# Twelve clamps of an int64-to-float32 decode, moved from VectorE to GpSimd

## The chip, the cores and the metric

The kernel runs on one core of a Trainium2 chip. Its engines are TensorE (PE in the profile; PEld is its weight load), VectorE (DVE), ScalarE (ACT), GpSimd (POOL) and SyncE (SP, which only issues transfers here). Each engine works through its own queue in order, and engines wait for one another by semaphores. The metric is the device time of one execution in microseconds, compared as the median of several runs.

## The reference, cut to what matters

Attention with a local band, global columns and distance biases (ALiBi), and behind it a two-layer MLP with a clipped gate:

```python
# q, k, v: (4, 8, 768, 64) float32; n_global 8, n_local 96; w_in (512, 2048), w_out (2048, 512)
scores = q @ k.T / 8 - slope[h] * dist      # masked to the band and the 8 global columns
a = softmax(scores); attn = a @ v
x = attn as (3072, 512)
h = x @ w_in
g = h * clip(h + 3, 0, 6) / 6
out = g @ w_out                             # float32, (3072, 512)
```

The weights reach the kernel as 64-bit words (float64 bits) of which the kernel makes float32 on the chip. This is the decoding that the change touches.

## The kernel before, in words

**Tiling.** The 3072 rows of x are eight blocks of 384 rows. In a block, attention is worked in four pairs of heads; pairs are numbered through all blocks, 0 to 31. The MLP of a block has 16 steps, f = 0 to 15, of 128 hidden units each. A step has two halves: twelve matmuls of 128x384 into the bank hp (L166), and nine of 128x512 into three accumulators (L198). Between the halves ScalarE and VectorE make the gate g (L177, L178), its high part gh (L186 on ScalarE, or L184 on GpSimd in later blocks) and the rest gl (L191). Each weight is kept as a high and a low part (w1h and w1l, w2h and w2l), hence three products per matmul.

**Weights.** They come in 32 chunks of 128x512 words, chunk 2f for the first half of step f and chunk 2f+1 for the second. A chunk's path is: a 512 KB transfer into a staging tile wst (L363, issued by SyncE); on ScalarE the magnitude of the high words, |high| into wz (L371); on GpSimd the low words scaled into we (L375); on VectorE the clamp of wz to the float32 exponents (L393), the mask and shift (L394), the sign (L402, which reads wst for the last time on VectorE), the sum with we (L408); on ScalarE the high part w1h or w2h (L412); on VectorE the low part w1l or w2l (L399). There are two buffers each of wst, wz and we, so the fetch of chunk i+2 waits for L402 and L375 of chunk i.

**The early part.** Blocks 0 to 2 get their attention (pairs 0 to 11) while the weights are decoded. Per pair: score matmuls (L809), distance and minimum on VectorE (L824), the exponentials on ScalarE (L828), sums on VectorE (L838, L839), division of the six row tiles n by their sums on GpSimd (L848; pair 0 on VectorE), transposes on TensorE (L856, L858) whose results ScalarE and VectorE copy to pt (L860), and the products with the values (L900) into one bank xp. ScalarE and VectorE bring that to xh (L152) and xl (L153); the next pair's L900 waits for xl, as there is one bank. From pair 8 on, steps f = 0 to 5 of block 0 stand between the pairs: hp of f0 ahead of pair 8's other transposes, and so on, f5 after pair 11's products. Then come steps 0 to 5 of block 1, steps 6 to 15 of blocks 0 and 1 in turn, and blocks 2 to 7, with the attention of the next block between their steps.

**What sets the order.** The generator `decode` yields after every part of a chunk with a price in microseconds of VectorE; `work` adds up the prices given to TensorE and to VectorE and takes further parts of the decoding as long as VectorE's account is the lower. That sets where in the program the parts stand. On TensorE, SyncE and GpSimd the queues keep program order (`in_order`); on VectorE and ScalarE a scheduler places the instructions. `magnitude(i + 1)` is called with L408 of chunk i.

```python
def work(self, pe, dve):
    self.given[0] += pe
    self.given[1] += dve
    while self.given[1] < self.given[0] and self.decoded < self.allowed:
        self.decode_step()
```

Of the kernel before, what the change touches and what calls it, by code (L numbers as in the profile page):

```python
# [9 lines left out]
F32 = mybir.dt.float32  # L10
# [4 lines left out]
ALU = mybir.AluOpType  # L15
# [23 lines left out]
LEAST, MOST = (float(np.uint32(e << 20).view(np.float32)) for e in (896, 1151))  # L39
# [10 lines left out]
FIRST = 6  # L50
# [8 lines left out]
class Kernel:  # L59
# [305 lines left out]
    def magnitude(self, i):  # L365


        words = self.raw[i].rearrange("p (c w) -> p c w", w=2)
        self.z[i] = self.zp.tile([P, DM], I32, name="wz")
        self.e[i] = self.ep.tile([P, DM], I32, name="we")  # L370
        self.nc.scalar.activation(out=self.z[i].bitcast(F32), in_=words[:, :, 1].bitcast(F32), func=AF.Abs)  # L371
        if i == 0:
            self.tc.add_manual_dep(self.nc.cur_bb.bb.instructions[-1], self.held, mybir.DependencyInfo(
                mybir.DependencyClass.NoSync, mybir.DependencyReason.DATA), reason="behind the first pairs")
        self.nc.gpsimd.tensor_scalar(out=self.e[i], in0=words[:, :, 0].bitcast(U32), scalar1=2.0 ** -29, scalar2=0.0, op0=ALU.mult, op1=ALU.add)  # L375

    def part(self, i, w1, w2):
        f = i // 2
        return (self.w1(w1, f), lambda a: a.rearrange("p (k c) -> p k c", k=NKT)) if i % 2 == 0 else (self.w2(w2, f), lambda a: a)

    def decode(self):

        nc = self.nc
        ts, stt, tt = nc.vector.tensor_scalar, nc.vector.scalar_tensor_tensor, nc.vector.tensor_tensor
        N = 2 * NF
        self.magnitude(0)
        for i in range(N + 1):
            a, b = i < N, i > 0  # L390
            if a:
                z = self.z[i]
                ts(out=z.bitcast(F32), in0=z.bitcast(F32), scalar1=LEAST, scalar2=MOST, op0=ALU.max, op1=ALU.min)  # L393
                ts(out=z, in0=z, scalar1=0x07FFFFFF, scalar2=3, op0=ALU.bitwise_and, op1=ALU.logical_shift_left)  # L394
            yield 0.68 * a
            if b:
                hi, sh = self.part(i - 1, self.w1h, self.w2h)
                lo, _ = self.part(i - 1, self.w1l, self.w2l)
                tt(out=lo, in0=sh(self.z.pop(i - 1).bitcast(F32)), in1=hi.bitcast(F32), op=ALU.subtract)  # L399
            yield 0.6 * b  # L400
            if a:
                stt(out=z, in0=self.raw[i].rearrange("p (c w) -> p c w", w=2)[:, :, 1], scalar=-0x40000000, in1=z,  # L402
                    op0=ALU.bitwise_and, op1=ALU.bitwise_or)
                if i + 2 < N:
                    self.fetch(i + 2)
            yield 0.6 * a
            if a:
                tt(out=z, in0=z, in1=self.e.pop(i), op=ALU.add)  # L408
                if i + 1 < N:
                    self.magnitude(i + 1)  # L410
                hi, sh = self.part(i, self.w1h, self.w2h)
                nc.scalar.copy(out=hi, in_=sh(z.bitcast(F32)))  # L412
            yield 0.69 * a
# [566 lines left out]
```

## Time and profile before

| What | Value |
|---|---|
| Median of three runs | 668.42 us (668.13 to 668.87) |
| The profiled execution's own time | 668.19 us |
| Its span, first to last instruction | 666.4 us |
| Granted TensorE clock | 0.999 |
| TensorE busy | 654.5 us, 98% of the span |
| VectorE busy | 423.4 us, 64% |
| ScalarE busy | 278.9 us, 42% |
| GpSimd busy | 219.9 us, 33% |

The span has 1.8 us less than the time of its execution; a change of the span is read as a change of the time. Busy time of TensorE is generous, since matmuls are pipelined and their ends are modelled; idle time is what is surely lost. The early part is told by stretches of 10 us, as the shares of the whole span say little of it. "SPq" rows are issues of transfers by SyncE, and the duration of such a row spans all its issues.

### The profile page before, as it was taken

What the parts mean: (1) busy time and instruction counts of PE and PEld (TensorE: products, weight loads), DVE (VectorE), ACT (ScalarE), POOL (GpSimd) and SP (SyncE); (2) the same over time, 40 slices, a digit from 0 to 9 for tenths busy, and PEclk for the clock granted to TensorE, in tenths of its full rate; (3) what the DMA queues carried; (4) which work ended last, traced back from release to release, by engine and by line L of the source; (5) the groups of instructions that cost most, each with busy time, mean ns of one, the idle gap of its engine ahead of it and who ended that gap; (6) DMA issues with size and microseconds to landing.
All of it is one profiled execution on the core that took longest, in us unless ns stands there. A gap on an engine that the chain in (4) does not pass through costs nothing.

```text
span 666.4 us, 11474 instructions
## 1 busy us (share of the span) xinstructions
PE 654.5 (98%) x3963; PEld 586.1 (88%) x3963; DVE 423.4 (64%) x1121; ACT 278.9 (42%) x736; POOL 219.9 (33%) x389
## 2 busy tenths in 40 slices
PE   9989999999999999999999999999999999999997
PEld 8768888888999999999999999899999999989995
DVE  6899999999234876366663886457662777422222
ACT  6898756555236333154324433143331444131111
POOL 5666622221000553043340444225340444302110
PEclk9999999999999999999999999999999999999999
DMA  8685644442003446625663366624555255510001
GB/s 288 179 253 195 198 150 135 153 134 94 1 1 134 135 139 184 174 81 138 164 154 131 86 179 164 173 80 126 155 152 137 80 150 147 138 48 2 1 1 53
DMA packets 60837, 84.74 MB, mean 127 GB/s; under 512 B 8416, under 2 KB 45536, under 8 KB 60768
## 3 DMA queue, kind: packets, MB, share of 16 engines
q1 hardware_dynamic: 60480, 83.64, 43.3%
q8 instruction: 33, 0.54, 0.3%
q14 instruction: 36, 0.29, 0.1%
q10 hardware_dynamic: 288, 0.26, 0.1%
HBM read 62.92 MB, written 20.97 MB: 126 GB/s over the span
## 4 chain that ended last, share of the span: by engine, by line
PE 81%; DVE 9%; ACT 3%; DMA 3%; issue 2%; POOL 1%; SPq 0%; ACTq 0%; DVEq 0%; POOLq 0%
PE hp L166 36%; PE acc L198 33%; DMA wst<-w 3%; PE xp L900 2%; PE sp L813 2%; PE tp L900 2%; PE tp L813 2%; ACT n L828 2%; DVE wz L402 2%; DVE wz L408 1%; DVE n L824 1%; DVE wz L394 1%; PE sp L198 1%; PE tp L198 1%; PE xp L198 1%
## 5 line engine op out<-in xcount | busy, mean ns | idle before, releaser
L177 ACT ACTIVATE g<-hp,small 128x384 f32<-128x384 f32 x127 | 73.5, 579 | 251.5 <-PE hp L166 231.9
L166 PE MATMUL hp<-xh,w1h 128*128 128x384 f32 x512 | 174.1, 340 | 0.8 <-ACT w1h L412 0.7
L166 PE MATMUL hp<-xh,w1l 128*128 128x384 f32 x512 | 172.9, 338 | 0.1
L166 PE MATMUL hp<-xl,w1h 128*128 128x384 f32 x512 | 172.0, 336 | 0.0
L184 POOL TENSOR_SCALAR gh<-g 128x384 fp32r<-128x384 f32 x96 | 51.6, 538 | 292.6 <-DVE g L178 257.4
L198 PE MATMUL acc<-w2h,gl 128*128 128x512 f32 x336 | 133.0, 396 | 0.1
L198 PE MATMUL acc<-w2l,gh 128*128 128x512 f32 x336 | 132.4, 394 | 0.0
L198 PE MATMUL acc<-w2h,gh 128*128 128x512 f32 x336 | 132.0, 393 | 0.0
L178 DVE SCALAR_TENSOR_TENSOR g<-g,hp 128x384 f32<-128x384 f32 x128 | 69.7, 544 | 86.7 <-ACT g L177 86.5
L848 POOL TENSOR_SCALAR n<-n,sums 128x232 f32<-128x232 f32 (+1 forms) x186 | 101.7, 562 | 35.7 <-DVE sums L839 21.3
L191 DVE TENSOR_TENSOR gl<-g,gh 128x384 fp32r<-128x384 f32 x128 | 78.6, 614 | 50.0 <-POOL gh L184 45.3
L828 ACT ACTIVATE n<-n,least 128x232 f32<-128x232 f32 (+1 forms) x192 | 89.1, 466 | 45.1 <-DVE least L824 43.9
L166 PEld LDWEIGHTS hp<-xh,w1h 128*128 128x128 f32 x512 | 96.3, 188 | 6.6 <-issue 1.4
L166 PEld LDWEIGHTS hp<-xl,w1h 128*128 128x128 f32 x512 | 96.2, 188 | 3.9
L166 PEld LDWEIGHTS hp<-xh,w1l 128*128 128x128 f32 x512 | 96.0, 188 | 0.4 <-DVE w1l L399 0.4
L198 PEld LDWEIGHTS acc<-w2h,gl 128*128 128x128 f32 x336 | 63.0, 187 | 14.7 <-DVE gl L191 1.0
L198 PEld LDWEIGHTS acc<-w2h,gh 128*128 128x128 f32 x336 | 63.3, 188 | 10.3 <-POOL gh L184 0.3
L198 PEld LDWEIGHTS acc<-w2l,gh 128*128 128x128 f32 x336 | 63.2, 188 | 10.3
L873 DVE STREAM_TRANSPOSE blocks<-n 128x256 f32<-128x256 f32 x112 | 43.5, 424 | 31.0 <-POOL n L848 18.7
L375 POOL TENSOR_SCALAR we<-wst 128x512 int32<-128x512 uint32 x32 | 27.8, 868 | 68.6 <-DMA wst<-w 52.2
L784 POOL TENSOR_SCALAR kx<-load 64x504 fp32r<-64x504 f32 (+1 forms) x40 | 31.0, 776 | 37.5 <-PE hp L166 35.9
L824 DVE CUSTOM_DVE_ANT_0 n<-sp,d 128x232 f32<-128x232 f32 (+1 forms) x70 | 23.6, 374 | 29.5 <-PE sp L813 29.0
(110 smaller groups left out, 780.9 us busy)
## 6 DMA issues: line engine op xcount, KB each, us to landing
wst<-w SPq DMA_DIRECT2D x32, 512.0 KB, 3.5
load<-pairs SPq DMA_DIRECT2D x22, 636.0 KB, 5.2
there<-blocks SPq DMA_DIRECT2D x52, 256.0 KB, 2.6
load<-pairs SPq DMA_DIRECT2D x32, 384.0 KB, 3.9
weights<-there SPq DMA_DIRECT2D x48, 192.0 KB, 3.8
out<-o SPq DMA_DIRECT2D x23, 256.0 KB, 2.1
weights<-there SPq DMA_DIRECT2D x32, 160.0 KB, 3.2
load<-pairs SPq DMA_DIRECT2D x9, 444.0 KB, 3.6
```

The costliest lines, as they stand in the source:

```text
L166: self.nc.tensor.matmul(hp, lhsT=self.w1(w, f)[:, kt, :], rhs=a[:, kt, :], start=(n == 0), stop=(n == 3 * NKT - 1))
L177: nc.scalar.activation(out=g, in_=hp, func=AF.Relu, bias=self.three, scale=1.0)
L178: nc.vector.scalar_tensor_tensor(out=g, in0=g, scalar=6.0, in1=hp, op0=ALU.min, op1=ALU.mult)
L184: self.nc.gpsimd.tensor_scalar(out=gh, in0=g, scalar1=1.0, scalar2=0.0, op0=ALU.mult, op1=ALU.add)
L191: self.nc.vector.tensor_tensor(out=gl, in0=g, in1=gh.bitcast(F32), op=ALU.subtract)
L198: self.nc.tensor.matmul(acc[tt], lhsT=a[:, tk], rhs=self.w2(w, f), start=(f == 0 and j == 0), stop=(f == NF - 1 and j == 2))
L375: self.nc.gpsimd.tensor_scalar(out=self.e[i], in0=words[:, :, 0].bitcast(U32), scalar1=2.0 ** -29, scalar2=0.0, op0=ALU.mult, op1=ALU.add)
L784: nc.gpsimd.tensor_scalar(out=part["kx"][own, c], in0=k[own, c], scalar1=1.0, scalar2=0.0, op0=ALU.mult, op1=ALU.add)
L824: nc.vector.tensor_tensor_reduce(out=e[:, j, lo:W], in0=sp[j][:, lo:W], in1=d, op0=ALU.add, op1=ALU.min, scale=scale, scalar=3.0e38, accum ...
L828: nc.scalar.activation(out=e[:, j, lo:W], in_=e[:, j, lo:W], func=AF.Exp, bias=self.least[:, i:i + 1], scale=-1.0, accum_out=self.sums[:, ...
L848: nc.gpsimd.tensor_scalar(out=e[:, j, lo:W], in0=e[:, j, lo:W], scalar1=over, scalar2=0.0, op0=ALU.mult, op1=ALU.add)
L873: nc.vector.transpose(out=blocks[:, :, s].rearrange("p b j q -> p j b q"), in_=e[:, :, c:c + P].rearrange("p j (b q) -> p j b q", b=4))
```

## The change

For the chunks i < 12 the clamp is no longer L393 on VectorE but a GpSimd instruction right behind the scaling of the low words (L378 in the new numbering), with the two bounds taken in the other order (minimum first). The price that `decode` yields for its first part falls from 0.68 to 0.34 for these chunks. Everything behind L375 gets line numbers 6 or 7 higher: L393, L394, L399, L402, L408 and L412 become L400, L401, L406, L409, L415 and L419; L824, L838, L839, L848 and L900 become L831, L845, L846, L855 and L907.

```diff
         self.nc.gpsimd.tensor_scalar(out=self.e[i], in0=words[:, :, 0].bitcast(U32), scalar1=2.0 ** -29, scalar2=0.0, op0=ALU.mult, op1=ALU.add)
+        if self.helped(i):
+            z = self.z[i].bitcast(F32)
+            self.nc.gpsimd.tensor_scalar(out=z, in0=z, scalar1=MOST, scalar2=LEAST, op0=ALU.min, op1=ALU.max)
+
+    def helped(self, i):
+        return i < 2 * FIRST
...
                 z = self.z[i]
-                ts(out=z.bitcast(F32), in0=z.bitcast(F32), scalar1=LEAST, scalar2=MOST, op0=ALU.max, op1=ALU.min)
+                if not self.helped(i):
+                    ts(out=z.bitcast(F32), in0=z.bitcast(F32), scalar1=LEAST, scalar2=MOST, op0=ALU.max, op1=ALU.min)
                 ts(out=z, in0=z, scalar1=0x07FFFFFF, scalar2=3, op0=ALU.bitwise_and, op1=ALU.logical_shift_left)
-            yield 0.68 * a
+            yield (0.34 if self.helped(i) else 0.68) * a
```

The lower price moves the decoding forward in the program. TensorE's order stays as it was. Three places show the rest.

GpSimd, from the chunks ahead of pair 10's division (n) to that of pair 11, before:

```order
L375 TENSOR_SCALAR we<-wst 128x512 x2
L848 TENSOR_SCALAR n<-n,sums 128x128 x2
L848 TENSOR_SCALAR n<-n,sums 128x232 x4
L375 TENSOR_SCALAR we<-wst 128x512 x2
L848 TENSOR_SCALAR n<-n,sums 128x128 x2
L848 TENSOR_SCALAR n<-n,sums 128x232 x4
```

and from the last chunk ahead of pair 10's division in the change:

```order
L375 TENSOR_SCALAR we<-wst 128x512
L378 TENSOR_SCALAR wz<-wz 128x512
L855 TENSOR_SCALAR n<-n,sums 128x128 x2
L855 TENSOR_SCALAR n<-n,sums 128x232 x4
L375 TENSOR_SCALAR we<-wst 128x512
L378 TENSOR_SCALAR wz<-wz 128x512
L375 TENSOR_SCALAR we<-wst 128x512
L378 TENSOR_SCALAR wz<-wz 128x512
L375 TENSOR_SCALAR we<-wst 128x512
L378 TENSOR_SCALAR wz<-wz 128x512
L855 TENSOR_SCALAR n<-n,sums 128x128 x2
L855 TENSOR_SCALAR n<-n,sums 128x232 x4
```

Before, chunks 4 and 5 stood ahead of pair 10 and chunks 6 and 7 ahead of pair 11. Now chunks 5 and 6 stand ahead of pair 10 (the first of them is not shown) and chunks 7, 8 and 9 ahead of pair 11, each with its clamp.

SyncE, the fetches of chunks (wst) and the value loads of pairs 11, 12 and 13 (768 wide), before:

```order
L290 DMA load_167<-pairs 128x768
L363 DMA wst<-w 128x1024 x2
L290 DMA load_72<-pairs 128x768
L363 DMA wst<-w 128x1024 x2
L290 DMA load_73<-pairs 128x768
L363 DMA wst<-w 128x1024 x21
```

and in the change:

```order
L290 DMA load_167<-pairs 128x768
L363 DMA wst<-w 128x1024 x3
L290 DMA load_72<-pairs 128x768
L363 DMA wst<-w 128x1024 x2
L290 DMA load_73<-pairs 128x768
L363 DMA wst<-w 128x1024 x19
```

The three fetches behind the first of these loads are those of chunks 8, 9 and 10; before, the two there were those of chunks 7 and 8, and chunk 9 stood behind the load of pair 12, which waits for pair 9's products.

VectorE, from xl of pair 9 to xl of pair 10 (both L153), before:

```order
L153 TENSOR_TENSOR xl<-xp,xh 128x384
L402 SCALAR_TENSOR_TENSOR wz<-wst,wz 128x512
L399 TENSOR_TENSOR w2l_143<-wz,w2h_142 128x512
L408 ISA wz<-wz,we 128x1024
L178 SCALAR_TENSOR_TENSOR g<-g,hp 128x384
L393 TENSOR_SCALAR wz<-wz 128x512
L394 TENSOR_SCALAR wz<-wz 128x512
L399 TENSOR_TENSOR w1l_141<-wz,w1h_140 128x4x128
L191 TENSOR_TENSOR gl<-g,gh 128x384
L402 SCALAR_TENSOR_TENSOR wz<-wst,wz 128x512
L393 TENSOR_SCALAR wz<-wz 128x512
L153 TENSOR_TENSOR xl<-xp,xh 128x384
```

and in the change the last twelve up to xl of pair 10 (seven more stand between the two xl):

```order
L406 TENSOR_TENSOR w1l_141<-wz,w1h_140 128x4x128
L401 TENSOR_SCALAR wz<-wz 128x512
L409 SCALAR_TENSOR_TENSOR wz<-wst,wz 128x512
L415 ISA wz<-wz,we 128x1024
L406 TENSOR_TENSOR w2l_143<-wz,w2h_142 128x512
L401 TENSOR_SCALAR wz<-wz 128x512
L409 SCALAR_TENSOR_TENSOR wz<-wst,wz 128x512
L415 ISA wz<-wz,we 128x1024
L401 TENSOR_SCALAR wz<-wz 128x512
L406 TENSOR_TENSOR w1l_141<-wz,w1h_140 128x4x128
L409 SCALAR_TENSOR_TENSOR wz<-wst,wz 128x512
L153 TENSOR_TENSOR xl<-xp,xh 128x384
```

xl of pair 10 now stands behind the sign (L409) of chunk 11; before, it stood behind the clamp of chunk 10.

## The prediction

> **What bounds the kernel now.** I read the stretches first, then what TensorE waits for, then the queues around the places where it waits.
>
> Stretches: us, then busy us (and instructions) of PE, PEld, DVE, ACT and POOL, granted clock, DMA share and GB/s.
>
> ```profile
> 20.00:30.00 10.00, 9.18 (x94) 7.14 (x92) 8.84 (x43) 8.76 (x34) 6.10 (x15) 1.00 0.71 202
> 30.00:40.00 10.00, 8.74 (x92) 6.97 (x90) 8.70 (x33) 9.23 (x31) 6.96 (x14) 1.00 0.75 218
> 40.00:50.00 10.00, 8.39 (x95) 6.75 (x95) 9.07 (x37) 9.23 (x34) 5.60 (x13) 1.00 0.89 267
> 50.00:60.00 10.00, 9.77 (x74) 8.72 (x73) 9.39 (x30) 8.82 (x27) 6.79 (x11) 1.00 0.57 166
> 60.00:70.00 10.00, 9.33 (x67) 8.21 (x67) 9.69 (x31) 8.55 (x26) 5.96 (x8) 1.00 0.72 250
> 70.00:80.00 10.00, 10.00 (x80) 8.57 (x80) 9.12 (x19) 6.89 (x14) 7.38 (x9) 1.00 0.61 180
> 80.00:90.00 10.00, 8.39 (x65) 6.94 (x62) 9.24 (x18) 6.53 (x13) 2.24 (x3) 1.00 0.53 163
> 90.00:150.00 60.00, 59.91 (x300) 53.60 (x299) 59.37 (x110) 34.78 (x61) 15.49 (x17) 1.00 0.43 142
> ```
>
> From 90 us on TensorE is idle for 0.09 us of 60, at full clock. VectorE is as full there, but a TensorE that never stops cannot be hurried, so only the first 90 us can give anything. There TensorE idles 0.82 + 1.26 + 1.61 + 0.23 + 0.67 + 0 + 1.61 = 6.2 us between 20 and 90. Whatever moves the point at which it gets to full rate, some 90 us in, moves the end by as much, as long as nothing new holds it behind.
>
> What TensorE waited for (total us, times, longest):
>
> ```profile
> PE xp L900 <- DVE xl L153: 3.3, 6, 1.0
> PE tp L856 <- ACT pt L860: 1.2, 2, 0.8
> PE hp L166 <- ACT w1h L412: 0.7, 1, 0.7
> PE sp L809 <- DVE least L824: 0.6, 1, 0.6
> ```
>
> So VectorE releases 3.9 us of the idling, ScalarE 1.9. The last two large waits come late, and the timeline of ScalarE shows why:
>
> ```profile
> 81.40 0.30 PE L856 MATMUL tp<-ident,n 128*128 128x128 f32 x1 [0.81 <-ACT pt L860]
> 88.17 0.45 PE L166 MATMUL hp<-xh,w1h 128*128 128x384 f32 x1 [0.69 <-ACT w1h L412]
> 74.43 3.54 SPq L363 DMA_DIRECT2D wst<-w  x2
> 74.43 4.64 DMA wst<-w
> 79.15 0.70 ACT L371 ACTIVATE wz<-wst 128x512 f32<-128x512 f32 x1 [1.62 <-DMA wst<-w]
> 80.68 0.57 ACT L860 COPY pt<-tp 128x512 f32<-128x512 f32 x1
> ```
>
> Chunk 9 is fetched at 74.43 and lands 4.64 us later, at 79.07; its magnitude (L371) had held ScalarE for 1.62 us, and the copy pt queued behind it came late. The decode is thus bound by its chain of fetch, ScalarE and VectorE with two buffers, not only by VectorE's time.
>
> **The change part by part.** *The clamps leave VectorE.* Group rows of wz and we, duration ns min/median/max:
>
> ```profile
> L393 DVE TENSOR_SCALAR wz<-wz x32: 406/416/841, 17.4 to 161.2; 128x512 f32<-128x512 f32 x32
> L394 DVE TENSOR_SCALAR wz<-wz x32: 410/424/871, 17.9 to 162.0; 128x512 int32<-128x512 int32 x32
> L375 POOL TENSOR_SCALAR we<-wst x32: 648/796/1711, 30.2 to 160.1; 128x512 int32<-128x512 uint32 x32
> ```
>
> Twelve of L393 at 0.416 us are 5.0 us of VectorE, spread over the early part.
>
> *They come to GpSimd.* No GpSimd clamp of this size is in the trace. Bounds: L375 has as many elements in one operand, 0.65 at the least and 1.71 at the most; I take its median, 0.8 us, so 9.6 us in all. It stands ahead of L401 (the mask) where VectorE's clamp stood, and needs both the magnitude from ScalarE and its turn behind L375. A chunk's path gets longer by 0.8 - 0.42 = 0.4 us, 1.1 where L375 of the same chunk is late too.
>
> *Two engines at once.* L394 takes 0.41 us at its fastest and 0.87 at its slowest. The difference, 0.46, bounds what one GpSimd instruction takes from VectorE from above; nothing bounds it from below. If every clamp cost that once, 12 x 0.46 = 5.5 us would eat the 5.0 us. I take half, so VectorE gains some 2 us and not 5.
>
> The Trainium skill's page SBUF — State Buffer, section Who interferes with whom, says that VectorE and GpSimd share one port pair, held as an exclusive lock for a whole instruction, so that the other is fully blocked. By that rule VectorE's gain would be about nil instead of 2 us; the doubled maximum of L394 agrees with it, the median of 0.424 says that it does not strike each time. On the other side the GPSIMD Engine Reference, section Engine selection, sends elementwise work to VectorE but calls one-input work roughly line rate on GpSimd, by which the clamp would be an estimated 0.42 us instead of 0.8, and my sum below 0.4 less; the rows of L393 and L375 (0.416 against 0.796) do not agree.
>
> *The decoding moves forward in the program.* This is the part that I think decides. GpSimd's queue keeps program order, and the division of pair 11 (six instructions) now stands behind chunks 7, 8 and 9 with their clamps, no longer behind chunks 6 and 7.
>
> ```profile
> 71.47 5.09 POOL L848 TENSOR_SCALAR n<-n,sums 128x128 f32<-128x128 f32 x6 [0.17 <-ACT wz L371]
> 73.48 0.68 DVE L402 SCALAR_TENSOR_TENSOR wz<-wst,wz 128x512 int32<-128x512 int32 x1
> 76.44 0.38 PE L856 MATMUL tp<-ident,n 128*128 128x128 f32 x2
> 86.16 1.32 PE L900 MATMUL xp<-pt,load 128*64 128x128 f32 x20
> ```
>
> Before, the division began at 71.47, and the transposes of its first two tiles ran at 76.44 with time to spare. Now it waits for chunk 9, step by step:
>
> 1. Chunk 9's buffer is free after L402 of chunk 7, which ended at 73.48 + 0.68 = 74.2. On VectorE the clamps ahead of it are gone, but each mask waits for GpSimd instead; SyncE no longer has a pair's load ahead of this fetch. I take the fetch at 73.7, between 72.2 (clamps of chunks 3 to 7 gone, 5 x 0.42) and 75.2 (the longer path, twice).
> 2. Landing: 4.64 us for this chunk before; the median of all fetches, in the row below, is 3.5. I take 4.3: 78.0.
>
> ```profile
> wst<-w SPq DMA_DIRECT2D x32, 512.0 KB, 3.5
> L848 POOL TENSOR_SCALAR n<-n,sums 128x128 f32<-128x128 f32 x30 | 14.7, 498 | 20.8 <-DVE sums L839 12.3 <-ACT g L177 3.9 <-DVE least L824 2.7
> ```
>
> 3. Magnitude 0.7 (ScalarE; L375 runs beside it): 78.7. Clamp 0.8, and 0.1 for the two hand-overs: 79.6. That is 8.1 us later than 71.47.
> 4. First tile of pair 11 divided, 0.5 to 0.85 (498 ns each, or a sixth of the 5.09 us): 80.3. TensorE keeps its order, so it stands at these transposes from about 76.4 on: **+3.9 us**, with 77.6 - 76.4 = +1.2 (72.2 + 3.5 + 0.7 + 0.65 + 0.1 + 0.5) and 83.2 - 76.4 = +6.8 (75.2 + 4.64 + 0.7 + 1.71 + 0.1 + 0.85) from the low and the high end of every step.
> 5. Given back: the waits at 81.40 (0.81) and 88.17 (0.69). Behind a late pair 11 ScalarE has had its copies done and chunks 9 and 10 are decoded in time: **-1.5 us**; at worst only the first, -0.8.
> 6. Taken again: xl of pair 10 stands behind the sign (L409) of chunk 11, and L900 of pair 11 needs it.
>
> ```profile
> 63.67 4.36 POOL L848 TENSOR_SCALAR n<-n,sums 128x128 f32<-128x128 f32 x6
> 75.73 0.54 DVE L153 TENSOR_TENSOR xl<-xp,xh 128x384 fp32r<-128x384 f32 x1
> L399 DVE TENSOR_TENSOR w1l<-wz,w1h x16: 671/680/943, 32.3 to 162.4; 128x512 fp32r<-128x512 f32 x16
> ```
>
>    From 79.6: division 4.4 us (as pair 10's) to 5.1, then L375 and clamp of chunks 10 and 11, 4 x 0.8, to 87.2 to 87.9; mask 0.42, low part 0.68, sign 0.68, xl 0.54: 89.5 to 90.2. L900 of pair 11 would be ready at 86.16 + 3.9 - 0.8 = 89.3. So 0.2 to 0.9; I take **+0.3**, as these parts overlap at their ends.
>
> The sum is 3.9 - 1.5 + 0.3 = +2.7 us. What VectorE gains earlier (2 us by 88 us) does not lower it, since step 4 is set by chunk 9 and not by when TensorE gets there; it is in step 1. Behind 90 us nothing changes: more of the decode is done by then, TensorE is the bound there, and the covers are the same. If VectorE had not been relieved there, it would cost nothing as TensorE idles 0.09 us.
>
> Against the profiled execution's own time that is 668.19 + 2.7 = 670.9. The median of the runs is 0.2 above that execution, so I predict **671.0 us** for the median.
>
> **The rivals.**
>
> *VectorE's relief is what counts: faster.* For it: VectorE is 88% to 97% busy from 20 to 90, and it releases 3.9 us of TensorE's waits. Against it: ScalarE is as full (9.23 of 10) from 30 to 50, the late waits are ScalarE's and the fetch's, and GpSimd takes part of the gain. Price: 5.0 us freed, of which at most the 3.9 us can come back; with three quarters of them and pair 11 on time, -3.0: 665.4. Condition: chunk 9 is clamped by 76.
>
> *The delay is swallowed: no change.* If the decoding, earlier in the program, also runs earlier in time, chunk 9 is fetched at 72.2 and lands in 3.5 us: step 4 gives +1.2, step 5 takes 1.5, step 6 is nil: -0.3. With the fetch half a microsecond later it is +0.2: 668.6. For it: SyncE's order, where chunk 9 no longer waits for pair 9's products. Against it: L402 of chunk 7 was at 73.48 with the buffer chain already running without a break.
>
> *The queue strikes twice: much slower.* VectorE's own order puts xl of pair 10 behind chunk 11, and GpSimd's puts chunk 11 behind pair 11. With the division at 81 (chunk 9 at the high end of two of its steps) L900 of pair 11 comes at 81 + 5.1 + 3.2 + 2.3 = 91.6 instead of 86.16, and 0.7 of it is given back at 88.17: +4.7: 673.1. It decides once chunk 9 lands after 79, about where it landed before (79.07), which speaks for it; that earlier fetches have one load less in their way speaks against it.
>
> That the clamps would not move is no case: twelve GpSimd rows stand in the order of the program.
>
> **How the numbers follow.** The forecast (pair 11 behind chunk 9, +1 to +4) 0.48; struck twice 0.18; swallowed 0.21; VectorE's relief 0.13. A difference of 0.2% (1.3 us) is about what a measurement of this kernel can tell from no change, so faster is below 667.1 and slower above 669.8. Faster: the relief's 0.12 and 0.02 of the swallowed, 0.14. Same: 0.18 of the swallowed, 0.05 of the forecast, 0.01 of the relief, 0.24. Slower: 0.43 and 0.18 and 0.01, 0.62. The forecast alone lies in 669.4 to 672.4. The range for eight in ten reaches into the cases on both sides: 667.2 to 673.4.
>
> **What would show it.** In the changed profile: POOL's division of pair 11 should begin near 79.6, with a clamp (L378) and the fetch of chunk 9 ahead of it; PE's transposes (L863) should show one wait of 3 to 4 us for POOL around 76 to 80; the waits at pt and w1h of 0.81 and 0.69 should be gone; PE should idle some 9 us between 20 and 95 instead of 6.2. The clamp should read 0.65 to 1 us. Step 4 is wrong if the division of pair 11 begins by 77; the claim on VectorE is wrong if the waits of L907 for xl fall from 3.3 to under 1.5; the whole is wrong if TensorE reaches its unbroken stretch before 89.

## The result, and the profile after

The changed kernel takes **676.47 us** (675.74 to 677.17, 4 runs) where the kernel before takes 668.64 (668.13 to 669.28): ratio **1.0116 [1.0099, 1.0134]**, 7.8 us slower. The forecast was 671.0, in a range from 667.2 to 673.4: the side was right, the size three times too small.

The profiled execution took 677.17 us, the slowest of the four. Its stretches answer to those of before; columns are us, busy us (and instructions) of PE, PEld, DVE, ACT and POOL, granted clock, DMA share and GB/s:

```profile
20.00:30.00 10.00, 10.00 (x104) 7.91 (x100) 7.00 (x33) 9.02 (x35) 5.85 (x14) 1.00 0.75 209
30.00:40.00 10.00, 7.90 (x81) 6.22 (x80) 9.47 (x34) 8.26 (x27) 8.93 (x15) 1.00 0.75 235
40.00:50.00 10.00, 8.78 (x93) 6.53 (x93) 10.00 (x43) 10.00 (x36) 5.66 (x11) 1.00 0.83 258
50.00:60.00 10.00, 10.00 (x83) 9.35 (x80) 7.28 (x25) 8.56 (x27) 8.16 (x15) 1.00 0.55 173
60.00:70.00 10.00, 10.00 (x71) 8.71 (x70) 9.68 (x28) 7.99 (x25) 8.47 (x11) 1.00 0.64 226
70.00:80.00 10.00, 5.64 (x45) 4.49 (x43) 8.67 (x15) 5.20 (x11) 4.30 (x6) 0.90 0.42 120
80.00:90.00 10.00, 7.22 (x39) 5.46 (x40) 6.20 (x9) 4.51 (x8) 9.12 (x12) 0.59 0.36 134
90.00:150.00 60.00, 59.17 (x309) 52.13 (x308) 58.85 (x110) 35.45 (x62) 14.50 (x16) 1.00 0.46 152
```

TensorE idles 2.10 + 1.22 = 3.3 us from 20 to 70 (4.6 before), then 4.36 us in one stretch and 2.78 in the next; the clock of the second is 0.59, where the kernel before had 1.00. What TensorE waited for (total us, times, longest):

```profile
PE tp L863 <- POOL n L855: 7.9, 2, 6.9
PE xp L907 <- issue: 1.9, 1, 1.9
PE sp L198 <- DVE gl L191: 0.7, 1, 0.7
PE xp L907 <- DVE xl L153: 0.2, 1, 0.2
```

The waits at pt and w1h of before have shrunk or gone; one wait of 6.9 us for GpSimd is new. The waits for xl have not shrunk as far as their row says. The profile found no releaser for 1.9 us at L907 ("issue"), but that L907, of pair 4, began 0.1 us after an xl had ended (37.62 + 0.47 = 38.09 in the chain of waits), at the place where the kernel before waited 1.05 us for xl:

```profile
38.19 1.54 PE L907 MATMUL xp<-pt,load 128*64 128x128 f32 x24 [1.89 <-issue]
```

```profile
37.62 0.47 DVE xl L153
```

GpSimd's timeline around the wait of 6.9 us (L375 low words, L378 the new clamp, L855 division), then the chain of waits (start, us, what), then TensorE's timeline:

```profile
74.31 0.94 POOL L378 TENSOR_SCALAR wz<-wz 128x512 f32<-128x512 f32 x1
80.18 0.64 POOL L375 TENSOR_SCALAR we<-wst 128x512 int32<-128x512 uint32 x1 [4.93 <-DMA wst<-w]
80.90 0.61 POOL L378 TENSOR_SCALAR wz<-wz 128x512 f32<-128x512 f32 x1
81.50 4.81 POOL L855 TENSOR_SCALAR n<-n,sums 128x128 f32<-128x128 f32 x6
```

```profile
74.91 5.10 DMA wst<-w
```

```profile
75.53 0.33 PE L166 MATMUL hp<-xh,w1l 128*128 128x384 f32 x1
82.74 0.99 PE L863 MATMUL tp<-ident,n 128*128 128x128 f32 x2 [6.87 <-POOL n L855]
83.95 0.63 PE L198 MATMUL acc<-w2l,gh 128*128 128x512 f32 x1
88.00 0.42 PE L865 MATMUL tp<-ident,n 128*128 128x128 f32 x1
95.63 0.45 PE L166 MATMUL hp<-xh,w1h 128*128 128x384 f32 x1
107.64 0.50 PE L198 MATMUL sp<-w2h,gl 128*128 128x512 f32 x1 [0.73 <-DVE gl L191]
```

GpSimd stands for 4.93 us waiting for chunk 9, with pair 11's division queued behind it; TensorE, done at 75.53 + 0.33 = 75.86, waits until 82.74. Then its matmuls are slow: 0.63 us for one of L198, a group of which takes 398 ns on the mean (busy us, mean ns, idle before). The clock in pieces of 2 us says when:

```profile
L198 PE MATMUL acc<-w2h,gl 128*128 128x512 f32 x336 | 133.8, 398 | 0.2
```

```profile
76.00:78.00 2.00, 0.00 (x0) 0.00 (x0) 1.75 (x4) 0.92 (x2) 0.00 (x0) 1.00 0.75 250
78.00:80.00 2.00, 0.00 (x0) 0.00 (x0) 1.29 (x3) 0.00 (x0) 0.00 (x0) 0.51 0.36 53
86.00:88.00 2.00, 2.00 (x7) 1.51 (x6) 0.22 (x1) 0.23 (x1) 1.72 (x4) 0.50 0.57 229
88.00:90.00 2.00, 2.00 (x26) 1.50 (x26) 1.93 (x3) 1.03 (x2) 1.66 (x2) 0.93 0.00 0
```

TensorE's last matmul ends at 75.86, and by about 78 the clock is at half; it is full again only after 88. The whole loss splits by the busy times at the head of each page (busy us, share, instructions); before, then after:

```profile
PE 654.5 (98%) x3963; PEld 586.1 (88%) x3963; DVE 423.4 (64%) x1121; ACT 278.9 (42%) x736; POOL 219.9 (33%) x389
```

```profile
PE 658.0 (97%) x3963; PEld 587.2 (87%) x3963; DVE 421.2 (62%) x1109; ACT 278.5 (41%) x736; POOL 230.2 (34%) x401
```

The span grew from 666.4 to 675.4 us, by 9.0. The same matmuls were busy 3.5 us longer, so TensorE's idling grew by 9.0 - 3.5 = 5.5. I use this split below.

### The profile page after: what moved, and what is told of

Its sections match the earlier page's. It is cut to its first block, busy times and chain, and to the rows that moved or that the text cites. A ratio compares the mean times of both kernels' runs of the same rounds, so it can differ in the third digit from the quotient of the medians.

```text
span 675.4 us, 11454 instructions
## 1 busy us (share of the span) xinstructions
PE 658.0 (97%) x3963; PEld 587.2 (87%) x3963; DVE 421.2 (62%) x1109; ACT 278.5 (41%) x736; POOL 230.2 (34%) x401
## 4 chain that ended last, share of the span: by engine, by line
PE 79%; DVE 9%; DMA 5%; ACT 3%; POOL 2%; issue 2%; SPq 0%; POOLq 0%; ACTq 0%; DVEq 0%
PE hp L166 34%; PE acc L198 32%; DMA wst<-w 5%; PE xp L907 2%; PE sp L820 2%; PE tp L907 2%; DVE wz L409 2%; PE tp L820 2%; ACT n L835 2%; DVE wz L415 1%; POOL n L855 1%; PE xp L358 1%; DVE wz L401 1%; DVE n L831 1%; DVE gl L191 1%
## 5 line engine op out<-in xcount | busy, mean ns | idle before, releaser
L177 ACT ACTIVATE g<-hp,small 128x384 f32<-128x384 f32 x127 | 73.7, 580 | 251.6 <-PE hp L166 230.5
L166 PE MATMUL hp<-xh,w1h 128*128 128x384 f32 x512 | 174.0, 340 | 0.0
L166 PE MATMUL hp<-xh,w1l 128*128 128x384 f32 x512 | 172.7, 337 | 0.0
L166 PE MATMUL hp<-xl,w1h 128*128 128x384 f32 x512 | 171.9, 336 | 0.0
L198 PE MATMUL acc<-w2h,gl 128*128 128x512 f32 x336 | 133.8, 398 | 0.2
L198 PE MATMUL acc<-w2l,gh 128*128 128x512 f32 x336 | 133.1, 396 | 0.0
L198 PE MATMUL acc<-w2h,gh 128*128 128x512 f32 x336 | 132.9, 395 | 0.0
L191 DVE TENSOR_TENSOR gl<-g,gh 128x384 fp32r<-128x384 f32 x128 | 80.6, 630 | 53.2 <-POOL gh L184 44.9
L855 POOL TENSOR_SCALAR n<-n,sums 128x232 f32<-128x232 f32 (+1 forms) x186 | 103.1, 570 | 31.2 <-DVE sums L846 17.6
L166 PEld LDWEIGHTS hp<-xh,w1h 128*128 128x128 f32 x512 | 96.3, 188 | 5.5 <-issue 1.5
L166 PEld LDWEIGHTS hp<-xl,w1h 128*128 128x128 f32 x512 | 96.2, 188 | 3.9
L166 PEld LDWEIGHTS hp<-xh,w1l 128*128 128x128 f32 x512 | 96.0, 188 | 0.0
L198 PEld LDWEIGHTS acc<-w2h,gl 128*128 128x128 f32 x336 | 63.4, 189 | 15.4 <-DVE gl L191 1.7
L198 PEld LDWEIGHTS acc<-w2h,gh 128*128 128x128 f32 x336 | 63.8, 190 | 10.4 <-POOL gh L184 0.3
L198 PEld LDWEIGHTS acc<-w2l,gh 128*128 128x128 f32 x336 | 63.6, 189 | 10.4
L375 POOL TENSOR_SCALAR we<-wst 128x512 int32<-128x512 uint32 x32 | 26.6, 832 | 64.6 <-DMA wst<-w 56.7
L831 DVE CUSTOM_DVE_ANT_0 n<-sp,d 128x232 f32<-128x232 f32 (+1 forms) x70 | 23.6, 374 | 29.6 <-PE sp L820 29.1
```

The source lines that it names most:

```text
L166: self.nc.tensor.matmul(hp, lhsT=self.w1(w, f)[:, kt, :], rhs=a[:, kt, :], start=(n == 0), stop=(n == 3 * NKT - 1))
L177: nc.scalar.activation(out=g, in_=hp, func=AF.Relu, bias=self.three, scale=1.0)
L191: self.nc.vector.tensor_tensor(out=gl, in0=g, in1=gh.bitcast(F32), op=ALU.subtract)
L198: self.nc.tensor.matmul(acc[tt], lhsT=a[:, tk], rhs=self.w2(w, f), start=(f == 0 and j == 0), stop=(f == NF - 1 and j == 2))
L831: nc.vector.tensor_tensor_reduce(out=e[:, j, lo:W], in0=sp[j][:, lo:W], in1=d, op0=ALU.add, op1=ALU.min, scale=scale, scalar=3.0e38, accum ...
L855: nc.gpsimd.tensor_scalar(out=e[:, j, lo:W], in0=e[:, j, lo:W], scalar1=over, scalar2=0.0, op0=ALU.mult, op1=ALU.add)
```

## Experiments

Each kernel was timed against the kernel before on its own chip (medians from 667.86 to 668.12 us). Spans and splits are of one profiled execution each, against the 666.4 us and 654.5 busy us of before.

**Is it the order in the queue? Three kernels.** The first has the change with the old price, so that pair 11's division stands behind chunks 6 and 7 again:

```diff
-            yield (0.34 if self.helped(i) else 0.68) * a
+            yield 0.68 * a
```

> The clamps of twelve chunks stay on GpSimd, but the price of the first part of a chunk is 0.68 again, so that pair 11's division stands behind chunks 6 and 7 on GpSimd, as before the change. Theory A (the place in GpSimd's queue costs the time): the wait of 6.87 us at the transposes of pair 11 falls to under 1 us, TensorE's clock stays at 1.00, 668 to 669.5 us. Theory B (the clamps on GpSimd cost it, by a longer path per chunk and by slowing VectorE): 674 us or more.

Measured: **674.46**, ratio 1.0095 [1.0076, 1.0114]. Theory A fell, B held. The stall at pair 11 is gone and 6 us are still lost. The largest wait of TensorE from 75 to 95 us, then rows of GpSimd, VectorE and TensorE, each from that kernel:

```profile
PE hp L166 <- ACT w1h L419: 3.9, 2, 2.6
```

```profile
72.68 3.88 POOL L855 TENSOR_SCALAR n<-n,sums 128x128 f32<-128x128 f32 x6
77.38 0.61 POOL L378 TENSOR_SCALAR wz<-wz 128x512 f32<-128x512 f32 x1
86.17 0.65 POOL L375 TENSOR_SCALAR we<-wst 128x512 int32<-128x512 uint32 x1 [4.83 <-DMA wst<-w]
```

```profile
80.29 0.44 DVE L401 TENSOR_SCALAR wz<-wz 128x512 int32<-128x512 int32 x1
81.67 0.68 DVE L409 SCALAR_TENSOR_TENSOR wz<-wst,wz 128x512 int32<-128x512 int32 x1
```

```profile
92.47 0.44 PE L166 MATMUL hp<-xh,w1h 128*128 128x384 f32 x1 [2.61 <-ACT w1h L419]
```

The places have changed. Now the division (72.68) stands ahead of chunk 8, so chunk 8's clamp comes at 77.38 and, with VectorE's other work, its mask (L401) at 80.29 and its sign (L409) at 81.67. VectorE's timeline of the kernel before, where the clamp needed no GpSimd, has these parts of chunk 8 five microseconds earlier, while GpSimd was dividing:

```profile
74.09 0.60 DVE L393 TENSOR_SCALAR wz<-wz 128x512 f32<-128x512 f32 x1
75.21 0.60 DVE L394 TENSOR_SCALAR wz<-wz 128x512 int32<-128x512 int32 x1
76.19 0.91 DVE L402 SCALAR_TENSOR_TENSOR wz<-wst,wz 128x512 int32<-128x512 int32 x1
```

The sign frees the staging buffer, so chunk 10 is fetched late too (landed 86.1), and steps 4 and 5 of the MLP wait for their weights, 3.9 us in two waits. The second of them is 2.61 us, and behind it the clock drops once more (0.83, 0.50 and 0.81 in the three stretches of 2 us from 92 to 98). In this execution it had dropped early as well, behind the wait of 1.9 us that ends at 38 (0.94 from 30 to 40 us, 0.89 from 40 to 50). Of the 6.4 us by which the span grew, 3.2 are longer matmuls, from both dips.

The second kernel is the one before with the new price alone, clamps on VectorE:

```diff
-            yield 0.68 * a
+            yield (0.34 if i < 2 * FIRST else 0.68) * a
```

> The clamps are on VectorE as before the change; only the price of the first part of chunks 0 to 11 is 0.34, so that pair 11's division stands behind chunks 7, 8 and 9 on GpSimd. Theory A: TensorE waits 4 to 6 us at the transposes of pair 11 and its clock drops, 672 to 677 us. Theory B: about the kernel before, 667.5 to 669.5 us.

Measured: **671.93**, 1.0055 [1.0035, 1.0075], just under theory A's range. Moving the work forward in the program costs 3.7 us by itself, and partly in the place that the prediction named, since its GpSimd too waits for chunk 9 before it divides pair 11:

```profile
77.18 0.66 POOL L375 TENSOR_SCALAR we<-wst 128x512 int32<-128x512 uint32 x1 [3.15 <-DMA wst<-w]
77.94 5.40 POOL L848 TENSOR_SCALAR n<-n,sums 128x128 f32<-128x128 f32 x6
```

It began at 77.94, against 81.50 with the clamps on GpSimd. TensorE's waits there are 1.04 and 0.74 us, not the 4 to 6 of theory A; the clock does drop behind them (0.83, 0.50 and 0.82 from 80 to 86). Another 1.4 us are idled from 100 to 200, where the kernel before idles 0.1. The third kernel is the change with pair 11's division issued ahead of chunks 8 and 9:

```diff
                             pairs[n + 1].sum_up()
+                            if n + 1 == EARLY - 1:
+                                for u in range(NT):
+                                    pairs[n + 1].normalize(u)
...
-                            if 2 <= n + 1 < EARLY:
+                            if 2 <= n + 1 < EARLY - 1:
                                 for u in range(NT):
```

> The changed kernel with one edit: the division of pair 11 is issued straight behind its sums and so stands on GpSimd behind chunk 7 and ahead of chunks 8 and 9. Theory A: the division starts some 7 us earlier, at about 73 us instead of 81.5, no wait over 1 us at the transposes, clock 1.00, and with what VectorE gains 666.5 to 669.5 us. Theory B: 674 us or more.

Measured: **673.71**, 1.0085 [1.0068, 1.0102]. Missed: the stall is gone, and the late weights take its place as in the first kernel (waits from 75 to 95 us):

```profile
PE hp L166 <- ACT w1h L419: 3.7, 2, 2.1
PE hp L166 <- DVE w1l L406: 1.3, 2, 0.9
```

So with twelve clamps in GpSimd's queue either the division waits for the chunks (7.8 us lost) or the chunks wait for the division (6.3 and 5.6 us).

**Is it the clock? Two kernels.** The change with dummy matmuls in the wait, whose bank the transposes overwrite; they add TensorE work and leave the output as it is. First 56:

```diff
+        if self.n == EARLY - 1 and t == 0:
+            any_ = kk.three.broadcast_to([P, P])
+            for _ in range(56):
+                nc.tensor.matmul(bank[:, 0:P], lhsT=any_, rhs=any_, start=True, stop=True)
```

> The changed kernel with 56 extra matmuls of 128x128 (some 6 us) on TensorE ahead of the first transposes of pair 11, into the bank that these overwrite; the division of pair 11 stays where it is. Theory A2 (TensorE's clock falls to 0.5 because it idles for 6.87 us, and costs 2.6 us behind that): the clock stays at 1.00 and the time falls by 2 to 2.6 us to 673.9 to 674.5 us. Rival A3 (the slow stretch from 82 to 88 us has another cause, such as data that come late): no change, 676.5 us.

Measured: **682.36**, 1.0215 [1.0198, 1.0232]. I had sized the filler wrongly: a row of TensorE's timeline shows two passes for each of the 56,

```profile
75.47 12.67 PE L864 MATMUL tp<-small 128*128 128x128 f32 x112
```

so it ran 12.7 us, past the point at which pair 11 was ready (its division began at 79.38), and cost time by itself. It only shows, in its profiled execution, that no half-rate stretch comes when TensorE is busy. The same with `range(24)`:

> The changed kernel with 24 dummy matmuls (128x128, float32, into the bank that the transposes overwrite) ahead of pair 11's first transposes; they add TensorE work and leave the output as it is. At the 0.22 us each that the run with 56 of them shows they take 5.4 us, 75.9 to 81.3, inside the wait that ended at 82.74. Theory clock (the wait also costs half rate from 78 to 88, 2.6 us of the 8.9 by pair 11's last transposes): no half-rate stretch of some us, and 673.5 to 675. Rival (the slower matmuls are hidden behind the late weights and gl that come next): 676 to 677, as the changed kernel.

Measured: **675.83**, 1.0118 [1.0101, 1.0135]. In the profiled execution the clock stayed at full rate through the stretch that had been at half:

```profile
78.00:80.00 2.00, 2.00 (x20) 2.00 (x19) 1.67 (x4) 1.60 (x3) 1.46 (x2) 1.00 0.44 57
82.00:84.00 2.00, 1.56 (x8) 1.31 (x9) 1.16 (x3) 1.38 (x3) 2.00 (x4) 1.00 0.32 69
```

and the ratio is that of the changed kernel (1.0116). It missed the clock theory's range (673.5 to 675) and is below the rival's by 0.2. With two intervals of 0.0017 a gain of 2.6 us is all but excluded, one of 1 us is not. The test is weaker than it looks, as only the profiled execution is known to have kept the clock: its mean granted clock is 0.999, and it took 675.54, 0.2 less than the fastest of the changed kernel; the other three have 0.996 and 0.997, between the changed kernel's 0.992 to 0.995 and the 0.998 to 1.000 of before. By the profiled executions the matmuls cost 661.0 - 654.5 = 6.5 us more than before, of which the dummies are 5.5, so 1.0 is left of the 3.5; the idling, with the 5.5 that the dummies filled, is 6.3 us longer than before where it was 5.5. The clock dip is real, but between these two executions a part of what it took is idled away when it is gone.

**Is it contention? One kernel.** The kernel before, and beside VectorE's clamps the same twelve on GpSimd on a tile nobody reads:

```diff
+        if i < 2 * FIRST:
+            if i == 0:
+                self.spare = self.const.tile([P, DM], F32, name="spare")
+                self.nc.gpsimd.memset(self.spare, 1.0)
+            z = self.spare
+            self.nc.gpsimd.tensor_scalar(out=z, in0=z, scalar1=MOST, scalar2=LEAST, op0=ALU.min, op1=ALU.max)
```

> The kernel before, with all its clamps on VectorE and its order, and beside them twelve clamps of the same size on GpSimd, behind L375, on a spare tile that nobody reads: extra work that changes no output. Theory contention (GpSimd's clamps slow VectorE and fill GpSimd's queue, and that is what the clamps cost once the order is as before): most of the 6 us of the run with the old price, 673 to 675. Theory chain (what costs is that a chunk's mask must wait until GpSimd's queue, with the divisions in it, gets to its clamp): 668 to 669.5, with the divisions of pair 11 up to 1.3 us later and nobody waiting for them.

Measured: **670.65**, 1.0048 [1.0033, 1.0064], between the two theories: 2.8 us by the medians for clamps on which nobody waits. The busy times of its page:

```profile
PE 654.5 (98%) x3963; PEld 586.0 (88%) x3963; DVE 427.0 (64%) x1121; ACT 278.9 (42%) x736; POOL 229.0 (34%) x402
```

VectorE has the same 1121 instructions as before and is busy 427.0 - 423.4 = 3.6 us longer, 0.3 us for each clamp (two other kernels with the same 1121 instructions and no extra GpSimd work read 422.9 and 423.7).

**Which clamps? Two kernels**, both with the old price, the change for six chunks only:

```diff
     def helped(self, i):
-        return i < 2 * FIRST
+        return i < FIRST
```

> The changed kernel with the old price for all chunks and the clamps of chunks 0 to 5 alone on GpSimd. Theory chain: the loss is made at chunk 8, whose clamp stands behind pair 11's division, so the six early ones cost nothing and keep what the run with the old price had gained by 51 to 72 us (0.8 us): 667 to 668.5. Rival (each clamp costs a like amount): half of 6, 670.5 to 672.

and the other six with `return FIRST <= i < 2 * FIRST`:

> The changed kernel with the old price and the clamps of chunks 6 to 11 alone on GpSimd. Theory chain: all or most of the loss of the run with the old price, 672.5 to 675, with the mask of chunk 8 at 79 to 81 where the kernel before had it at 75.2. Rival (each costs a like amount): 670.5 to 672.

Measured: the first six **670.15**, 1.0032 [1.0022, 1.0042]; the last six **673.66**, 1.0086 [1.0069, 1.0103]. The last six alone cost nearly what all twelve cost at the old price, in the places named, with chunk 8's mask at 78.52 (the largest wait from 75 to 95 us):

```profile
PE hp L166 <- ACT w1h L419: 2.9, 2, 1.5
```

That the first six would be free was wrong by 2 us: their early gain (TensorE is 0.9 to 1.2 us ahead at 51 us) is 0.3 at pair 10's products (78.97 against 79.27), and pair 11's come 0.5 later than before (86.69 against 86.16).

**Which link of the chain? Four kernels.** The first gives the change at the old price a third staging buffer:

```diff
-            self.decoding(words, 2, 2, side="right")
+            self.decoding(words, 3, 2, side="right")
...
                 self.fetch(1)
+                self.fetch(2)
...
-                if i + 2 < N:
-                    self.fetch(i + 2)
+                if i + 3 < N:
+                    self.fetch(i + 3)
```

> The changed kernel with the old price for all chunks and a third staging buffer, so that chunk i+3 (not i+2) is fetched behind the sign of chunk i. Theory fetch (with the old price the weights of steps 4 and 5 come late because each fetch waits for a sign that is itself late: chunk 10 landed at 86.1 instead of 81.4): its waits at L166 go, 669 to 671. Theory queue (chunk 8 had landed by 75.9, and its clamp waited for GpSimd behind pair 11's division, its mask for VectorE until 80.3): most of the loss stays, 672.5 to 675.

The second takes pair 11's division off GpSimd instead:

```diff
-            if self.n == 0:
+            if self.n in (0, EARLY - 1):
                 nc.vector.tensor_scalar(out=e[:, j, lo:W], in0=e[:, j, lo:W], scalar1=over, scalar2=None, op0=ALU.mult)
```

> The changed kernel with the old price for all chunks and pair 11's division on VectorE (six instructions, 4 x 0.337 + 2 x 0.281 = 1.9 us by pair 0's rows) instead of GpSimd (3.9 to 5.1 us). Theory queue: chunk 8's clamp no longer stands behind the division, its mask comes by 77 instead of 80.3, the waits for the weights of steps 4 and 5 (3.9 us) shrink to under 1.5, and the time is 668 to 670.5. Theory chain (the way of a chunk over ScalarE, GpSimd and VectorE is itself too long, and the two engines slow each other): 672 to 675, with those waits still there.

The controls are the same two edits on the kernel before:

> The kernel before with pair 11's division on VectorE, the control for the run with the clamps on GpSimd. VectorE gets 1.9 us more at 71 to 76, where it is full, GpSimd gets rid of 5: both theories 667.5 to 669.5.

> The kernel before with a third staging buffer, the control for the run with the clamps on GpSimd. The late waits at pt (0.81) and w1h (0.69), put down to chunk 9's landing at 79.07, can go: 666.9 to 668.2. If VectorE sets the decode's pace anyway: 667.5 to 669.

| kernel | clamps on GpSimd, old price | clamps on VectorE |
|---|---|---|
| as it is | 1.0095 [1.0076, 1.0114] | 1 |
| third buffer | 669.90, 1.0025 [1.0013, 1.0036] | 670.08, 1.0029 [1.0020, 1.0039] |
| pair 11's division on VectorE | 670.87, 1.0045 [1.0028, 1.0061] | 669.77, 1.0023 [1.0013, 1.0033] |

Either edit takes most of the 6.3 us away: 4.4 the third buffer, 3.5 the division, with chunk 8's mask at 77.5 instead of 80.3, though that time stayed 0.4 us over its range. Both controls cost something in the kernel before, which I had not expected of either (the third buffer 2.1 us; the trace shows longer waits at pt and xl, whose cause stays open). Beside its control the third buffer leaves nothing of the loss; the division leaves 1.1 us. The waits at L166 did not go as the theory of the fetch had it (3.3 us are left), but TensorE gets to them early: step 5's weights let it start at 88.42, where the old price with two buffers had 92.47 and the kernel before 88.17, and the clock stays at 1.00.

```profile
88.42 0.45 PE L166 MATMUL hp<-xh,w1h 128*128 128x384 f32 x1 [1.11 <-ACT w1h L419]
```

**Is the stall in the changed kernel the same thing? Two kernels.** The changed kernel with its new price and order, and a third buffer by the edit above:

> The changed kernel (new price, clamps on GpSimd, pair 11's division behind chunks 7, 8 and 9) with a third staging buffer, so that chunk 9 is fetched behind the sign of chunk 6 (about 69.5) and not of chunk 7 (74.9). Theory fetch: chunk 9 has landed by 75, pair 11's division begins at 76 to 77.5 instead of 81.5, the wait of 6.87 at its transposes shrinks under 2, and the time is 669 to 671.5. Rival (order: the chunks ahead of the division cost GpSimd and VectorE as much whenever they are fetched): 673 or more.

and this with pair 11's division first, by the edit of the third kernel:

> The same with a third staging buffer and pair 11's division issued straight behind its sums, ahead of chunks 8 and 9. Theory fetch: with two buffers this order lost 5.6 us to late weights of steps 4 and 5; with three these waits (3.7 and 1.3) go, and nothing stands ahead of the division: 667.5 to 669.5, the best of the kernels with all twelve clamps on GpSimd. Rival (the way of a chunk over three engines still makes the weights late): 670 to 672.

Measured: **671.02**, 1.0045 [1.0028, 1.0062], and **669.12**, 1.0013 [1.0003, 1.0023]. The first has the changed kernel's order in GpSimd's queue, and its timelines of GpSimd and TensorE show the division 4 us earlier:

```profile
77.35 4.30 POOL L856 TENSOR_SCALAR n<-n,sums 128x128 f32<-128x128 f32 x6
```

```profile
77.78 0.33 PE L864 MATMUL tp<-ident,n 128*128 128x128 f32 x1 [1.98 <-POOL n L856]
78.95 0.33 PE L864 MATMUL tp<-ident,n 128*128 128x128 f32 x1 [0.85 <-POOL n L856]
```

It is 4.8 us faster than the changed kernel against before. The longest wait is under 2 us as expected, the two together are 2.8. The second is the best of those with twelve clamps on GpSimd, and no faster than the kernel before. Of its ten executions the two with a mean granted clock of 0.999 took 667.45 and 668.03, the other eight, at 0.994 to 0.997, took 668.29 to 669.71. What is left of the loss there goes with the clock, though no run changes the clock alone. None of the fourteen kernels beats the one before.

## Why the prediction was right or wrong

**What held.** The mechanism and its place: pair 11's division behind chunk 9's clamp, one wait of TensorE at L863, the waits at pt and w1h gone, and 2.10 + 1.22 + 4.36 + 2.78 = 10.5 us of idling from 20 to 90 (some 9 to 95 were forecast). The clamp's group row (ns: least, median, most) has 0.94 us in the middle, where I took 0.8:

```profile
L378 POOL TENSOR_SCALAR wz<-wz x12: 615/937/1155, 29.9 to 88.8; 128x512 f32<-128x512 f32 x12
```

GpSimd's busy time rose by 230.2 - 219.9 = 10.3 us where the sum had 9.6. The run with the new price alone shows the stall, weaker, without the clamps' own work; the run with a third buffer in the changed kernel shows that the fetch makes the larger part of it.

**VectorE's gain of 2 us instead of 5** held by the busy times: 423.4 - 421.2 = 2.2 us. The spare clamps gave 0.3 us of slowing per clamp, 3.6 in all, where the step took half of 0.46, 2.8 in all. The Trainium skill's page SBUF — State Buffer, section Who interferes with whom, gives the shared port pair for a whole instruction to whichever of the two engines issues first and blocks the other, where the VectorE instruction uses that pair. The twelve spare clamps ran 0.61 to 1.12 us each and cost VectorE 0.3 on the mean, so the trace agrees with a shared resource; no run shows which instructions were blocked. Single rows go beyond the bound of 0.46: the sign (L409) takes 0.68 us in the middle and 1.20 at most. The test that I had named for this step, waits of L907 for xl under 1.5 us, reads 0.2 by the row; with the 1.89 us that the profile puts down to "issue" it is 2.1, and the test does not strike. What VectorE gained came to nothing in the time, because TensorE was early at pair 11 (75.86 against 76.44) and stood there. (VectorE's least share from 20 to 90 us was 8.70 of 10, 87% and not 88%; nothing hangs on it.)

**What failed is the size of step 4, by its steps 1 and 2, and a term that the sum did not have.**

| step | forecast | profile after |
|---|---|---|
| 1: fetch of chunk 9 | 73.7 | 74.91 |
| 2: landing | 4.3 us | 5.10 us |
| 3: division begins | 79.6 | 81.50 |
| 4: pair 11's first transposes, against 76.44 | +3.9 | 82.74: +6.3 |
| half clock until 88 | none | +2.6 |
| 5: given back by 88.17 of before | -1.5 | 95.63: +7.46, so -1.5 |
| 6: xl of pair 10 | +0.3 | no wait at L907 of pair 11 (94.38) |
| behind that, what remains of the span | 0 | +1.5 |
| sum | +2.7 | +9.0 (span) |

Step 1 assumed that a chunk taken up earlier in the program is fetched earlier. It isn't: its fetch waits for the sign of chunk 7, which ended at 73.64 + 1.13 = 74.77 in this row of VectorE's timeline (74.16 before). The chain through GpSimd's queue ate what the order had gained: chunk 7's magnitude was done at 69.74 + 0.68 = 70.42, but its clamp began at 71.91, behind the division of pair 10. And the sign itself took 1.13 us beside GpSimd's work, where it had taken 0.68:

```profile
73.64 1.13 DVE L409 SCALAR_TENSOR_TENSOR wz<-wst,wz 128x512 int32<-128x512 int32 x1
```

The landing of 5.10 us lies above anything I allowed. It is no outlier: the fetch at 57.16 took 5.33 us in the profile of the kernel before, and my high end (4.64) left that one out. The 82.74 still lies under step 4's own high end, 83.2, which the range of the whole did not carry. In the two runs with dummy matmuls, whose decode has the same order, the division began earlier (79.38 in the first), so part of this is scatter, and the profiled execution is the slowest of its four; the medians differ by 7.8 and not 9.0.

The **clock** has no term in the sum. The last transposes behind those of pair 11's first tiles ran at 88.00; TensorE's timeline of the kernel before has them at 79.07:

```profile
79.07 0.27 PE L858 MATMUL tp<-ident,n 128*128 128x128 f32 x1
```

That is 8.9 us late, 2.6 more than at 82.74, and between them TensorE ran without a break at half rate. It adds up in the profile, but the kernel whose profiled execution kept the clock was no faster in the median, so I cannot call these 2.6 us a cause of the measured 7.8: how much of them counts stays open. **Behind 90 us nothing changes** was wrong as well: gl came 0.73 us late at 107.64, and TensorE idles 0.83 us from 90 to 150 instead of 0.09; that is about half of the +1.5, and the rest is not traced.

**What the prediction missed altogether** is that the stall hides a second loss of the same size. I costed the change as one delay in GpSimd's queue; with that delay taken out (the first and the third kernel) 5.6 to 6.3 us stay: the weights of steps 4 and 5 come late (step 5 starts at 92.47 and 91.79 instead of 88.17, 4.3 and 3.6 us), and the clock drops behind that. The longer path of a chunk was in my working only as 0.4 to 1.1 us on one fetch. It closes a loop: a later clamp makes a later sign, that a later fetch of the chunk after next, and that the next late clamp. The third buffer cuts this loop, and takes 4.4 to 4.8 us out of all three orders (1.0116 to 1.0045, 1.0095 to 1.0025, 1.0085 to 1.0013), although in the kernel before it costs 2.1.

**The rivals.** VectorE's relief and the swallowed delay fell. *The queue strikes twice*, 673.1, had its condition met, since chunk 9 landed at 74.91 + 5.10 = 80.01 and it decided from 79 on, but its mechanism, xl of pair 10 late at L907, did not show: pair 11's L907 began at 94.38 without a wait, and the 0.2 us in the row of xl were waited at 31.35.

## What to carry to other kernels

When an operation moves to another in-order queue, cost not only its time there but what stands ahead of it: here a 0.9 us clamp came to stand in series with divisions of 4 to 5 us, and either order lost 5.6 to 7.8 us. If the moved step releases a buffer whose next load feeds the same step, follow the delay once round the loop; another buffer is the test that shows whether that loop is the cause. And a stall found by its row may be hiding a second one: take it away before crediting it with the whole loss.

## What the runs showed of the hardware

The granted clock fell to half sooner than I would have guessed. In the changed kernel it was 0.51 by 78 to 80 us, some 2 us after the last matmul, and after the matmuls began again at 82.7 it took until 88 to recover. The kernel with a third buffer and pair 11 first shows it behind a wait of 2.2 us; these are its waits and its clock:

```profile
PE tp L867 <- ACT pt L871: 2.2, 1, 2.2
```

```profile
80.00:90.00 10.00, 7.92 (x48) 7.14 (x49) 8.96 (x16) 6.08 (x12) 2.83 (x4) 0.83 0.65 225
```

A wait of 1.98 us (the changed kernel with a third buffer, at 77.78) did not bring it; in the run with the new price alone two shorter ones a little apart (1.04 and 0.74 us) did. All ten kernels with the first six clamps on GpSimd have a wait of 1.9 us that ends near 38: behind it three of the profiled executions show the lower clock (0.50 to 0.57 from 40 to 42 us, with the old price, with pair 11 first, and in the changed kernel with a third buffer), and the other seven do not. So it is no fixed length of one wait; what else decides stays open. The Trainium skill's page TensorE: Matmul & The Clock Gate, section Part 1: The HAM clock gate, puts the fall behind an idle window of about 3.4 us and the recovery behind as much of sustained work; here about 2 us were enough for the fall, and the recovery took 5.3 in the changed kernel.
